# Folding the cosine and sine matrices into w_in with half-width pairs of matmuls, and one fold and one conversion at another place in the order

## The chip, the cores and the metric

The kernel runs on one core of a Trainium2 chip. The metric is device time of one execution in microseconds (us); lower is better. TensorE multiplies matrices into banks of PSUM; VectorE, ScalarE and GpSimd work on tiles element by element; SyncE issues the DMAs. Every engine works through its own queue in order, and instructions on different engines wait for each other through semaphores.

## The reference

```python
X = np.fft.fft(np.fft.fft(x, axis=1), axis=2)      # x: 8 x 3008 x 256, fp32
h = X.real.reshape(8 * 3008, 256) @ w_in           # w_in: 256 x 2048
g = np.where(h >= 1, h, np.where(h <= -1, 0, (h + 1) ** 2 / 4))
return g @ w_out                                   # w_out: 2048 x 256
```

## The kernel before

**The sequence transform.** The length 3008 is 64 x 47, and both factors are done as matmuls against cosine and sine blocks (stage1 for 47, stage2 for 64). The result of one batch lies in tiles pqh and pql, a value and what is left of it after rounding to fp32r, in three chunks (k = 0, 1, 2) of 482, 512 and 512 columns.

**The model dimension.** The second transform, of length 256, is never done on x. It is linear, so its cosine and sine matrices (`mats`, 256 rows by 128 columns each) are multiplied into w_in once, at the start: that is the fold, `fold_w_in`. w_in is 256 x 2048 and is folded in four quarters of 512 columns (f4 = 0 to 3), each for m = 0 (cosine) and m = 1 (sine). Each of these takes two fp32 matmuls (line 317), one for each half h of the 256 rows, into one bank `wps`. The result is split into wh (ScalarE, line 242) and wl (VectorE, line 244). For m = 1 row 0 holds something else: ScalarE copies it out (`drow`, line 323), it goes through DRAM to `delta`, and GpSimd clears the row in wh and wl with two memsets (line 335) after wl is done. The DRAM bytes of w_in and w_out arrive as 64-bit integers, so each piece (raw_0 to raw_15) is converted first: ScalarE `magnitude` (lines 279, 281), VectorE `assemble` (lines 290, 294).

**The units.** The large part of the kernel is 384 units. A unit is one batch, one chunk k and one f, which is 128 of the 2048 hidden columns. Its steps are:
- G: six fp32r matmuls (line 477) into two banks uv_i_0 and uv_i_1, out of three banks of that tag;
- U, H: VectorE us (line 492) and the sum and difference h (lines 500, 501); h has three buffers;
- R, Q: ScalarE relu (line 506) and square (line 510);
- L: VectorE larger (line 521), min and max in place in h;
- J: ScalarE gh (line 525); T and t: the two halves of GpSimd gl (line 530), four buffers each;
- M: twelve fp32r matmuls (line 631) into four banks acc, which are copied out after the last f of a visit (lines 616, 618).

Because uv_i_0 and uv_i_1 come from three banks, a unit's matmuls wait for us or h of the unit before or the one before that; and because h has three buffers, h_17 waits until gl_14 has read h_14. Batch 0 is done in two visits, f 0 to 7 and then f 8 to 15, with units 0 to 7 on k = 0, 8 to 15 on k = 1, 16 to 23 on k = 2, and 24 on with f from 8. So quarter 0 of w_in is needed by unit 0, quarter 1 by unit 4, quarter 2 by unit 24 and quarter 3 by unit 28.

**The order.** Up to unit 47 the order of every instruction on TensorE, ScalarE, VectorE and GpSimd is written out by hand in the text `WRITTEN` (lines 73 to 101). A letter is a step, the number its index, and a point with a number the next piece of a step begun before: e and v are the two parts of a conversion, b and a the folds for m = 1 and m = 0 (b2 the matmuls, b2.1 and b2.2 what follows on the other engines), p the pieces of batch 0's transform (p8 the matmul ny, p8.1 the copy nyt on ScalarE), o the split of w_out, d the first delta; G, U, H, R, Q, L, J, T, t, M as above. All engines share the text: each takes from it, in order, what is its own. The banks of a fold and of a transform come from `fft_bank`, which hands out acc0 to acc3 in turn for the first `EARLY_BANKS` calls and the bank "fft" after that, and from `fold_bank`, which gives quarters 2 and 3 a bank of uv.

Of the kernel before, what the change touches and what calls it, by code (L numbers as in the profile page):

```python
# [72 lines left out]
WRITTEN = """
f0 f1 f2 f3 f4 f5 f6 f7 p0 p1 w2 e0 e1 p0.1 p1.1 v0 v1 b0 b0.1 b0.2 a0 a0.1 a0.2 k0 p3 p3.1 p2 p2.1 p4 p5 p4.1 p6
p6.1 e4 v4 p5.1 p7 p7.1 e5 v5 n0 n0.1 p9 p9.1 p9.2 p8 e2 v2 p10 p10.1 p10.2 b1 b1.1 b1.2 d0 d0.1 o2 G0 G0.1 G1
U0 H0 U1 p8.1 e3 v3 o2.1 R0 a1 a1.1 a1.2 Q0 L0 o3 J0 G1.1 H1 p11 p11.1 G2 U2 G2.1 G3 G3.1 p11.2 H2 T0 t0 M0 R1
Q1 L1 R2 J1 T1 t1 Q2 e6 U3 H3 R3 L2 J2 l12 G4 G4.1 G5 U4 v6 H4 M1 Q3 R4 Q4 o3.1 G5.1 p12 G6 U5 L3 J3 L4 U6 T2
t2 M2 G6.1 G7 o6 J4 p12.1 T3 l8 t3 M3 T4 t4 o6.1 H5 R5 l9 Q5 p12.2 G7.1 H6 G8 U7 G8.1 R6 e7 Q6 L5 J5 T5 t5 H7
R7 v7 o7 L6 U8 M4 p13 o7.1 M5 Q7 p13.1 p13.2 L7 J6 J7 T6 t6 T7 t7 H8 p14 p14.1 G9 G9.1 G10 U9 H9 G10.1 U10
p14.2 R8 Q8 R9 Q9 e8 H10 L8 L9 J8 T8 R10 M6 G11 M7 G11.1 G12 M7.1 U11 M7.2 v8 U12 G12.1 M7.3 M7.4 Q10 J9 t8 M8  # L80
e9 H11 L10 J10 G13 U13 G13.1 T9 t9 H12 M9 T10 t10 v9 H13 R11 R12 Q11 Q12 L11 L12 R13 G14 U14 b2 G14.1 M10 G15
J11 T11 t11 Q13 L13 M11 J12 b2.1 T12 t12 H14 U15 b2.2 l10 G15.1 G16 R14 J13 l13 Q14 T13 t13 H15 a2 G16.1 L14
U16 H16 a2.1 R15 J14 M12 Q15 L15 a2.2 R16 J15 e12 Q16 T14 t14 G17 U17 G17.1 H17 R17 Q17 M13 v12 e13 G18 X0 U18
G18.1 G19 T15 t15 L16 H18 R18 v13 X1 L17 M14 M15 M15.1 J16 T16 Q18 t16 U19 M15.2 b3 L18 G19.1 G20 M15.3 H19
M15.4 M16 J17 T17 t17 y1 J18 b3.1 b3.2 U20 G20.1 G21 a3 H20 G21.1 R19 Q19 L19 U21 M17 T18 t18 H21 X3 G22 G22.1
M18 R20 J19 Q20 L20 R21 a3.1 U22 a3.2 G23 J20 Q21 l11 T19 y0 t19 H22 T20 t20 X2 y2 G23.1 l15 G24 M19 M20 U23
L21 H23 e11 R22 J21 Q22 T21 t21 v11 R23 o11 Q23 G24.1 o11.1 l14 L22 J22 T22 t22 q0 G25 q0.1 U24 H24 G25.1 R24
G26 Q24 U25 e10 L23 J23 H25 M21 G26.1 G27 L24 v10 J24 R25 T23 t23 o10 e14 M22 M23 o10.1 T24 t24 Q25 U26 G27.1
H26 G28 v14 q1 R26 o14 o14.1 M23.1 M23.2 U27 Q26 X5 H27 q1.1 G28.1 G29 X4 q2 L25 L26 J25 J26 T25 t25 U28 M23.3
M23.4 M24 H28 T26 t26 y3 y4 y5 R27 Q27 R28 q2.1 L27 Q28 J27 e15 G29.1 M25 G30 M26 U29 G30.1 U30 L28 J28 T27  # L90
t27 T28 t28 X6 H29 R29 Q29 H30 X7 R30 v15 Q30 L29 L30 o15 J29 J30 T29 t29 o15.1 G31 M27 G31.1 q3 M28 U31 H31
G32 U32 G32.1 H32 q3.1 R31 Q31 L31 R32 Q32 L32 J31 G33 U33 G33.1 q4 q4.1 J32 D0 G34 M29 T30 t30 M30 T31 t31 T32
t32 H33 R33 Q33 G34.1 G35 U34 H34 R34 Q34 G35.1 U35 H35 R35 L33 L34 J33 J34 T33 t33 D1 Q35 M31 M31.1 M31.2 M31.3
M31.4 G36 q5 G36.1 G37 q5.1 U36 U37 H36 M32 M33 y6 R36 Q36 L35 L36 J35 J36 y7 T34 t34 T35 t35 q6 G37.1 G38
G38.1 U38 q6.1 M34 G39 M35 H37 H38 R37 Q37 R38 Q38 L37 L38 J37 J38 G39.1 z0 U39 G40 U40 T36 t36 M36 z0.1 T37 t37 T38
t38 G40.1 H39 H40 R39 Q39 L39 R40 Q40 J39 G41 U41 G41.1 G42 q7 M37 H41 R41 Q41 L40 J40 M38 q7.1 U42 L41 G42.1
G43 z1 G43.1 U43 J41 T39 t39 M39 T40 t40 T41 t41 z1.1 q8 H42 H43 R42 Q42 M39.1 M39.2 M39.3 L42 R43 J42 G44 G44.1
G45 q9 Q43 q9.1 U44 M39.4 M40 H44 R44 Q44 q9.2 U45 L43 M41 q10 G45.1 J43 L44 q10.1 q10.2 J44 G46 G46.1 U46 T42
t42 H45 T43 R45 t43 Q45 T44 H46 M42 t44 L45 R46 J45 G47 Q46 T45 G47.1 U47 M43 t45 L46 H47 J46 T46 R47 t46 Q47
M44 L47 J47 M45 T47 t47 q11 q11.1 q11.2  # L100
"""
# [671 lines left out]
```

## Time and profile before

| | |
|---|---|
| runs | 1715.49, 1716.52, 1718.16 us, median 1716.52 us |
| profiled execution | 1716.01 us, of which the span of the trace 1713.9 us |
| TensorE busy | 1703.1 us, 99% |
| VectorE, ScalarE, GpSimd busy | 80%, 79%, 70% |
| granted TensorE clock | 1.00 |
| DMA | 72.6 MB, mean 42 GB/s |

The span runs from the first to the last instruction that the profiler saw. "Idle before" an instruction, in brackets behind a row of the timeline, is the time in which its engine stood still, with what ended it. A row with x4 stands for four instructions one after the other, and its time for the stretch that they fill. A fp32 matmul leaves two records, a fp32r matmul one; records overlap a little, so the step from one start to the next is the better price.

### The profile page before, as it was taken

Reading aid. Unit: us, or ns where it says so; the run is one execution under the profiler, and the core shown is the slowest. Engines: PE = TensorE matmul, PEld = TensorE weight load, DVE = VectorE, ACT = ScalarE, POOL = GpSimd, SP = SyncE. Lnnn points to the kernel's source line nnn. Section 1 sums busy time; section 2 is a strip of 40 time slices with the busy share of each in tenths; the row PEclk is TensorE's granted clock in tenths of the full one; section 3 lists DMA queues with packets and bytes.
Section 4 is the critical chain, followed back from the end, with each engine's and each line's share of the span. In section 5 each row is a group of like instructions: output and inputs, shape, how many; then the busy total and the mean of one; then the engine's idle time right before and its main releaser. Section 6 shows DMA issues by size and latency. Waiting matters only on the chain.

```text
span 1713.9 us, 21467 instructions
## 1 busy us (share of the span) xinstructions
PE 1703.1 (99%) x7764; PEld 1402.0 (82%) x7764; DVE 1378.0 (80%) x1683; ACT 1354.2 (79%) x1576; POOL 1202.1 (70%) x852
## 2 busy tenths in 40 slices
...
DMA packets 34221, 72.64 MB, mean 42 GB/s; under 512 B 5312, under 2 KB 10432, under 8 KB 34115
## 3 DMA queue, kind: packets, MB, share of 16 engines
...
q8 instruction: 61, 1.00, 0.2%
...
HBM read 43.44 MB, written 27.82 MB: 42 GB/s over the span
## 4 chain that ended last, share of the span: by engine, by line
PE 79%; POOL 9%; issue 4%; ACT 4%; DVE 3%; DMA 1%; SPq 0%; POOLq 0%; DVEq 0%; ACTq 0%
PE acc L631 49%; PE uv L477 25%; POOL gl L530 7%; PE s L357 2%; PE s L426 2%; DVE h L521 2%; ACT gh L525 1%; ACT a L510 1%; ACT a L506 1%; POOL y L150 1%; DVE h L501 1%; DVE h L500 0%; DMA raw<-in_moe_w_in_dram 0%; DVE us L492 0%; PE wps L317 0%
## 5 line engine op out<-in xcount | busy, mean ns | idle before, releaser
L530 POOL TENSOR_TENSOR gl<-h,gh 128x512 fp32r<-128x512 f32 (+1 forms) x764 | 1101.2, 1465 | 479.6 <-ACT gh L525 459.6
L521 DVE SCALAR_TENSOR_TENSOR h<-a,h 128x1024 f32<-128x1024 f32 (+1 forms) x385 | 561.3, 1459 | 237.9 <-ACT a L510 237.5
L525 ACT ACTIVATE gh<-h 128x1024 fp32r<-128x1024 f32 (+1 forms) x385 | 400.8, 1041 | 306.4 <-DVE h L521 276.0
L631 PE MATMUL acc<-gh,woh 128*128 128x512 f32 (+1 forms) x1536 | 606.1, 395 | 1.3 <-ACT o L616 1.2
L631 PE MATMUL acc<-gl,woh 128*128 128x512 f32 (+1 forms) x1536 | 601.8, 392 | 1.0 <-POOL gl L530 0.8
L631 PE MATMUL acc<-gh,wol 128*128 128x512 f32 (+1 forms) x1536 | 595.2, 388 | 0.0
L506 ACT ACTIVATE a<-h,half 128x1024 f32<-128x1024 f32 (+1 forms) x385 | 431.9, 1122 | 23.6 <-DVE h L501 20.8
L510 ACT ACTIVATE a<-a 128x1024 f32<-128x1024 f32 (+1 forms) x385 | 399.2, 1037 | 7.8
L631 PEld LDWEIGHTS acc<-gl,woh 128*128 128x128 f32 x1536 | 288.4, 188 | 63.1 <-POOL gl L530 2.4
L631 PEld LDWEIGHTS acc<-gh,wol 128*128 128x128 f32 x1536 | 289.2, 188 | 60.6 <-POOL wol L244 0.4
L631 PEld LDWEIGHTS acc<-gh,woh 128*128 128x128 f32 x1536 | 289.1, 188 | 58.3 <-ACT o L616 2.9
L500 DVE TENSOR_TENSOR h<-us,uv 128x512 f32<-128x512 f32 (+1 forms) x384 | 259.5, 676 | 65.6 <-POOL gl L530 22.4
L477 PE MATMUL uv<-pqh,wh 128*128 128x512 f32 (+1 forms) x768 | 306.1, 399 | 0.9 <-DVE h L501 0.7
L477 PE MATMUL uv<-pql,wh 128*128 128x512 f32 (+1 forms) x768 | 301.5, 393 | 0.0
L477 PE MATMUL uv<-pqh,wl 128*128 128x512 f32 (+1 forms) x768 | 298.5, 389 | 0.0
L492 DVE SCALAR_TENSOR_TENSOR us<-nyb,delta,uv 128x512 f32<-128x512 f32 (+1 forms) x384 | 278.8, 726 | 3.7 <-PE uv L477 3.4
L501 DVE TENSOR_TENSOR h<-us,uv 128x512 f32<-128x512 f32 (+1 forms) x384 | 256.3, 667 | 0.0
L477 PEld LDWEIGHTS uv<-pqh,wh 128*128 128x128 f32 x768 | 144.3, 188 | 39.1 <-DVE h L501 7.1
L477 PEld LDWEIGHTS uv<-pql,wh 128*128 128x128 f32 x768 | 144.2, 188 | 31.8
L477 PEld LDWEIGHTS uv<-pqh,wl 128*128 128x128 f32 x768 | 144.2, 188 | 30.7 <-issue 1.2
L378 ACT ACTIVATE z<-s 64x192 f32<-64x192 f32 x244 | 82.8, 340 | 3.8 <-PE s L357 0.4
L150 POOL TENSOR_TENSOR y<-x 128x384 f32<-128x384 f32 x56 | 80.5, 1439 | 1.1 <-PE s L357 1.1
...
## 6 DMA issues: line engine op xcount, KB each, us to landing
...
```

What stands on the lines that cost most here:

```text
L150: nc.gpsimd.tensor_tensor(y, t[:, 0], t[:, 1], op=ALU.add)
L378: nc.scalar.activation(dst, src, AF.Copy)
L477: nc.tensor.matmul(t[:, :n], w[m][:, cols], r[:, m, :n], start=(j == 0), stop=(j == 2))
L492: fixed(i, nc.vector.scalar_tensor_tensor(us, nyb[b, k][:, :n], d, uv[0], op0=ALU.mult, op1=ALU.add), 2)
L500: fixed(i, nc.vector.tensor_tensor(h[:, 0], us, v, op=ALU.subtract), 2)
L501: fixed(i, nc.vector.tensor_tensor(h[:, 1], us, v, op=ALU.add), 2)
L506: fixed(i, nc.scalar.activation(a[:, sl], h[:, sl], AF.Relu, bias=half, scale=0.5), 2)
L510: fixed(i, nc.scalar.activation(a[:, sl], a[:, sl], AF.Square), 2)
L521: fixed(i, nc.vector.scalar_tensor_tensor(h[:, sl], a[:, sl], 1.0, h[:, sl], op0=ALU.min, op1=ALU.max))
L525: fixed(i, nc.scalar.activation(gh[:, sl], h[:, sl], AF.Copy))
L530: fixed(i, eng.tensor_tensor(gl[:, sg], h[:, sg], gh[:, sg].bitcast(F32), op=ALU.subtract))
L631: nc.tensor.matmul(acc[:, :n], w[:, f, wc], g[:, sg], start=(first and j == 0), stop=(last and j == 2))
```

## The change

1. G_ORDER, the order of the 128 cosine frequencies, now has the even ones first and the odd ones last; stage1 writes z in the same order.
2. For quarters 1, 2 and 3 the two halves of w_in's rows are added and subtracted on GpSimd before the fold (`sum_w_in`, letter s, two operations of 128 x 512). An even frequency needs only the sum and an odd one only the difference, so each m takes two matmuls of 64 output columns, one into each half of the bank, in place of two of 128 that add up. Quarter 1's sum is written over the spent raw_5, quarters 2 and 3 use a tile `sums`.
3. Banks: quarters 2 and 3 take "fft" for m = 1 and uv for m = 0; EARLY_BANKS goes from 15 to 17, and quarter 1's m = 1 and m = 0 now take acc0 and acc1; acc1 is the bank of ny.
4. Order: quarter 1's fold (b1, a1) stands behind H0; the conversion e2 v2 is spread behind unit 0's first steps; nyt (p8.1) stands behind R0; b2 and a2 stand together behind M11, b3 and a3 together between uv_23_0 and uv_23_1.

```diff
-G_ORDER = np.arange(P).reshape(XC, GPC, 2, 2).transpose(0, 3, 1, 2).reshape(-1)
+G_ORDER = np.arange(P).reshape(XC, GPC, 2, 2).transpose(3, 0, 1, 2).reshape(-1)
...
-p6.1 e4 v4 p5.1 p7 p7.1 e5 v5 n0 n0.1 p9 p9.1 p9.2 p8 e2 v2 p10 p10.1 p10.2 b1 b1.1 b1.2 d0 d0.1 o2 G0 G0.1 G1
+p6 p6.1 e4 v4 p5.1 p7 p7.1 e5 v5 s1 n0 n0.1 p9 p9.1 p9.2 p8 p10 p10.1 p10.2 d0 d0.1 G0 e2 G0.1 U0 G1 H0 b1 a1 U1
...
-EARLY_BANKS = 15
+EARLY_BANKS = 17
...
-    def fold_bank(f4, name):
-        if f4 < 2:
-            return fft_bank(0, name)
+    def fold_bank(f4, m, name):
+        if f4 < 2 or m:
+            return fft_bank(f4 // 2, name)
         return ps.tile([P, CH], F32, tag="uv", name=name, bufs=3)
...
         for h in range(2):
-            nc.tensor.matmul(pt, mats[m][h], f32s[4 * f4 + h], start=(h == 0), stop=(h == 1))
+            if f4 not in sums:
+                nc.tensor.matmul(pt, mats[m][h], f32s[4 * f4 + h], start=(h == 0), stop=(h == 1))
+            else:
+                g = slice(h * P // 2, (h + 1) * P // 2)
+                nc.tensor.matmul(pt[g], mats[m][0][:, g], sums[f4][h], start=True, stop=True)
...
+    def sum_w_in(f4):
+        lo, hi = f32s[4 * f4], f32s[4 * f4 + 1]
+        if f4 == 1:
+            total = spent.pop(4 * f4 + 1).rearrange("p e two -> p (e two)")[:, :CH].bitcast(F32)
+            sums[f4] = total, hi
+        else:
+            if not spare:
+                spare.append(sb.tile([P, NC, P + 1], F32, tag="z", name="sums", bufs=1).rearrange("p c n -> p (c n)"))
+            sums[f4] = [spare[0][:, (2 * (f4 % 2) + h) * CH :][:, :CH] for h in range(2)]
+        for t, op in zip(sums[f4], (ALU.add, ALU.subtract)):
+            nc.gpsimd.tensor_tensor(t, lo, hi, op=op)
...
-                dst = z[m * NA : (m + 1) * NA, :, (2 * q + h) * 8 : (2 * q + h + 1) * 8]
+                dst = z[m * NA : (m + 1) * NA, :, (XC * h + q) * 8 : (XC * h + q + 1) * 8]
```

What this does to an engine's queue shows in three places. The first is VectorE from us_1 to h_1, before:

```order
L492 SCALAR_TENSOR_TENSOR us_1_309<-nyb_0_0_247,delta_75,uv_1_0_299 128x482
L290 SCALAR_TENSOR_TENSOR cv_2_260<-cv_2_260,raw_3_114 128x512
L294 SCALAR_TENSOR_TENSOR cv_2_260<-raw_3_114,cv_2_260 128x512
L244 TENSOR_TENSOR wl0_71<-wps_1_0_325,wh0_69 128x512
L521 SCALAR_TENSOR_TENSOR h_0_305<-a_0_308,h_0_305 128x2x482
L500 TENSOR_TENSOR h_1_340<-us_1_309,uv_1_1_336 128x482
```

And the same stretch of VectorE after (cv is the converted w_in, wps_1_0 and wps_1_1 the banks of quarter 1's fold; larger 0 is the row that writes h_0 with 128x2x482):

```order
L512 SCALAR_TENSOR_TENSOR us_1_302<-nyb_0_0_249,delta_75,uv_1_0_288 128x482
L292 SCALAR_TENSOR_TENSOR cv_2_279<-cv_2_279,raw_2_112 128x512
L296 SCALAR_TENSOR_TENSOR cv_2_279<-raw_2_112,cv_2_279 128x512
L244 TENSOR_TENSOR wl1_72<-wps_1_1_296,wh1_70 128x512
L244 TENSOR_TENSOR wl0_71<-wps_1_0_299,wh0_69 128x512
L541 SCALAR_TENSOR_TENSOR h_0_292<-a_0_295,h_0_292 128x2x482
L292 SCALAR_TENSOR_TENSOR cv_2_279<-cv_2_279,raw_3_114 128x512
L296 SCALAR_TENSOR_TENSOR cv_2_279<-raw_3_114,cv_2_279 128x512
L520 TENSOR_TENSOR h_1_342<-us_1_302,uv_1_1_338 128x482
```

The conversion of raw_2 and wl1 have come into this stretch, and the conversion of raw_3 has moved from ahead of larger 0 to between larger 0 and h_1.

The second place is TensorE around unit 15 and 16, first before:

```order
L631 MATMUL acc_8_3_734<-gl_11_831,woh_73 128x512
L477 MATMUL uv_15_1_871<-pqh_0_1_344,wh1_70 128x512
...
L477 MATMUL uv_16_0_875<-pql_0_2_585,wh0_69 128x512
L317 MATMUL wps_2_0_892<-cv_8_657,cm_68 128x512 x2
L477 MATMUL uv_16_1_895<-pqh_0_2_584,wh1_70 128x512
```

And after:

```order
L651 MATMUL acc_8_3_736<-gl_11_833,woh_73 128x512
L323 MATMUL wps_2_1_862<-sums_792,cm_68 64x512 x2
L323 MATMUL wps_2_0_865<-sums_792,cm_68 64x512 x2
L497 MATMUL uv_15_1_870<-pqh_0_1_346,wh1_70 128x512
...
L497 MATMUL uv_16_0_874<-pql_0_2_587,wh0_69 128x512
L497 MATMUL uv_16_1_893<-pqh_0_2_586,wh1_70 128x512
```

Both folds of quarter 2 stand directly behind M11 (the rows that write acc_8); before, one stood between uv_16_0 and uv_16_1 and the other ahead of M10.

The third place is GpSimd between unit 11 and unit 14, first before:

```order
L530 TENSOR_TENSOR gl_11_831<-h_11_750,gh_11_830 128x512 x2
L530 TENSOR_TENSOR gl_12_850<-h_12_770,gh_12_849 128x512 x2
L335 MEMSET wh1_70 1x512
L335 MEMSET wl1_72 1x512
L530 TENSOR_TENSOR gl_13_881<-h_13_790,gh_13_880 128x512 x2
L530 TENSOR_TENSOR gl_14_909<-h_14_860,gh_14_908 128x512 x2
```

And after:

```order
L351 TENSOR_TENSOR sums_792<-cv_8_659 128x512 x2
L550 TENSOR_TENSOR gl_11_833<-h_11_752,gh_11_832 128x512 x2
L550 TENSOR_TENSOR gl_12_852<-h_12_772,gh_12_851 128x512 x2
L550 TENSOR_TENSOR gl_13_880<-h_13_795,gh_13_879 128x512 x2
L355 MEMSET wh1_70 1x512
L355 MEMSET wl1_72 1x512
L550 TENSOR_TENSOR gl_14_912<-h_14_856,gh_14_911 128x512 x2
```

The two sums stand ahead of gl_11, and the two clears of row 0, which wait for wl1, stand ahead of gl_14 and no longer ahead of gl_13.

## Rows read from the trace of the kernel before

**Rows 1.** The page's busy times: us, share of the span, instructions.

```profile
PE 1703.1 (99%) x7764; PEld 1402.0 (82%) x7764; DVE 1378.0 (80%) x1683; ACT 1354.2 (79%) x1576; POOL 1202.1 (70%) x852
```

**Rows 2.** The windows: from:to, length, busy time by engine, clock, DMA.

```profile
250.00:1700.00 1450.00, 1448.74 (x6620) 1202.03 (x6619) 1163.40 (x1403) 1143.45 (x1295) 1027.45 (x713) 1.00 0.09 30
```

**Rows 3.** TensorE's waits: us in total, times, longest us.

```profile
PE acc L631 <- ACT o L616: 1.2, 2, 0.7
PE s L426 <- DVE wl L244: 1.1, 1, 1.1
```

**Rows 4.** Groups of instructions, the fold: busy us, mean ns, idle before.

```profile
L317 PE MATMUL wps<-cv,cm 128*128 128x512 f32 x32 | 15.2, 599 | 1.0 <-DVE cv L294 1.0
```

**Rows 5.** The timeline of TensorE, 22 to 37 us: start, us, instruction.

```profile
23.04 0.31 PE L389 MATMUL ny<-cs,z 128*24 128x64 f32 x2
23.28 1.16 PE L426 MATMUL s<-cs,z 128*128 128x128 f32 x8
24.28 1.88 PE L317 MATMUL wps<-cv,cm 128*128 128x512 f32 x4
26.09 1.10 PE L341 MATMUL dps<-half,drow 1*128 1x64 f32 x8
27.12 0.49 PE L477 MATMUL uv<-pqh,wh 128*128 128x482 f32 x1
...
32.82 1.16 PE L426 MATMUL s<-cs,z 128*128 128x128 f32 x8 [1.07 <-DVE wl L244]
...
35.15 0.45 PE L477 MATMUL uv<-pqh,wh 128*128 128x482 f32 x1
...
36.54 0.38 PE L631 MATMUL acc<-gh,woh 128*128 128x482 f32 x1
```

**Rows 6.** The timeline of VectorE, 28 to 37 us.

```profile
28.16 0.72 DVE L492 SCALAR_TENSOR_TENSOR us<-nyb,delta,uv 128x482 f32<-128x482 f32 x1
...
30.75 0.69 DVE L290 SCALAR_TENSOR_TENSOR cv<-cv,raw 128x512 uint32<-128x512 uint32 x1
...
32.76 1.17 DVE L521 SCALAR_TENSOR_TENSOR h<-a,h 128x964 f32<-128x964 f32 x1
...
34.40 0.65 DVE L501 TENSOR_TENSOR h<-us,uv 128x482 f32<-128x482 f32 x1
```

**Rows 7.** The timeline of ScalarE, 26 to 36 us.

```profile
27.82 0.20 ACT L392 ACTIVATE nyt<-ny 24x64 f32<-24x64 f32 x1
...
30.24 1.10 ACT L506 ACTIVATE a<-h,half 128x964 f32<-128x964 f32 x1 [1.11 <-DVE h L501]
```

**Rows 8.** The timeline of TensorE, 80 to 118 us.

```profile
81.55 1.88 PE L317 MATMUL wps<-cv,cm 128*128 128x512 f32 x4
...
88.58 0.39 PE L631 MATMUL acc<-gl,woh 128*128 128x512 f32 x1
...
91.61 1.88 PE L317 MATMUL wps<-cv,cm 128*128 128x512 f32 x4
...
113.67 0.39 PE L631 MATMUL acc<-gh,woh 128*128 128x512 f32 x1
```

**Rows 9.** The timeline of VectorE, 78 to 118 us.

```profile
82.27 2.35 DVE L521 SCALAR_TENSOR_TENSOR h<-a,h 128x1024 f32<-128x1024 f32 x2
...
92.84 2.97 DVE L521 SCALAR_TENSOR_TENSOR h<-a,h 128x1024 f32<-128x1024 f32 x1 [0.39 <-ACT a L510]
...
112.26 0.68 DVE L618 COPY o<-acc 128x512 f32<-128x512 f32 x1
```

**Rows 10.** The timeline of GpSimd, 74 to 104 us (second row: 86.2 to 87).

```profile
84.87 6.04 POOL L530 TENSOR_TENSOR gl<-h,gh 128x512 fp32r<-128x512 f32 x4 [3.83 <-ACT gh L525]
...
86.11 2.29 POOL L530 TENSOR_TENSOR gl<-h,gh 128x512 fp32r<-128x512 f32 x1
...
91.25 0.52 POOL L335 MEMSET wh<- 1x512 f32 x1 [0.34 <-DVE wl L244]
...
92.20 2.53 POOL L530 TENSOR_TENSOR gl<-h,gh 128x512 fp32r<-128x512 f32 x2
```

More of the change, by code (lines that the diff above doesn't have):

```diff
@@ L79 @@
[L79 to L93, printed above, removed]
@@ L99 @@
-t42 H45 T43 R45 t43 Q45 T44 H46 M42 t44 L45 R46 J45 G47 Q46 T45 G47.1 U47 M43 t45 L46 H47 J46 T46 R47 t46 Q47
-M44 L47 J47 M45 T47 t47 q11 q11.1 q11.2
+f0 f1 f2 f3 f4 f5 f6 f7 p0 p1 w2 e0 e1 p0.1 p1.1 v0 v1 b0 b0.1 b0.2 a0 a0.1 a0.2 k0 p3 p3.1 p2 p2.1 p4 p5 p4.1
+p6 p6.1 e4 v4 p5.1 p7 p7.1 e5 v5 s1 n0 n0.1 p9 p9.1 p9.2 p8 p10 p10.1 p10.2 d0 d0.1 G0 e2 G0.1 U0 G1 H0 b1 a1 U1
+R0 v2 p8.1 b1.1 b1.2 Q0 a1.1 a1.2 o2 L0 e3 v3 o2.1 J0 o3 G1.1 H1 p11 p11.1 G2 U2 G2.1 G3 G3.1 p11.2 H2 T0 t0 M0
+R1 Q1 L1 R2 J1 T1 t1 Q2 e6 U3 H3 R3 L2 J2 l12 G4 G4.1 G5 U4 v6 H4 M1 Q3 R4 Q4 o3.1 G5.1 p12 G6 U5 L3 J3 L4 U6 T2
@@ new lines @@
+t2 M2 G6.1 G7 o6 J4 p12.1 T3 l8 t3 M3 T4 t4 o6.1 H5 R5 l9 Q5 p12.2 G7.1 H6 G8 U7 G8.1 R6 e7 Q6 L5 J5 T5 t5 H7 R7
+v7 o7 L6 U8 M4 p13 o7.1 M5 Q7 p13.1 p13.2 L7 J6 J7 T6 t6 T7 t7 H8 p14 p14.1 G9 G9.1 G10 U9 H9 G10.1 U10 p14.2 R8
+Q8 R9 Q9 e8 H10 L8 L9 J8 T8 R10 M6 G11 M7 G11.1 G12 M7.1 U11 M7.2 v8 U12 G12.1 M7.3 M7.4 Q10 J9 t8 M8 e9 H11 L10
+J10 G13 U13 G13.1 T9 t9 H12 M9 T10 t10 v9 s2 H13 R11 R12 Q11 Q12 L11 L12 R13 G14 U14 G14.1 M10 G15 J11 T11 t11
+Q13 L13 M11 J12 T12 t12 H14 U15 b2 a2 l10 G15.1 G16 R14 J13 l13 Q14 a2.1 T13 t13 H15 a2.2 G16.1 L14 U16 H16 b2.1
@@ new lines @@
+R15 J14 M12 Q15 L15 b2.2 R16 J15 e12 Q16 T14 t14 G17 U17 G17.1 H17 R17 Q17 M13 v12 e13 G18 X0 U18 G18.1 G19 T15
+t15 L16 H18 R18 v13 X1 L17 M14 M15 M15.1 J16 T16 Q18 t16 U19 M15.2 L18 G19.1 G20 M15.3 H19 M15.4 M16 J17 T17 t17
+y1 J18 U20 G20.1 G21 H20 G21.1 R19 Q19 L19 U21 M17 T18 t18 s3 H21 X3 G22 G22.1 M18 R20 J19 Q20 L20 R21 U22 G23
+b3 a3 J20 Q21 l11 T19 y0 t19 H22 a3.1 T20 t20 X2 y2 G23.1 l15 a3.2 G24 M19 M20 U23 b3.1 L21 b3.2 H23 e11 R22 J21
+Q22 T21 t21 v11 R23 o11 Q23 G24.1 o11.1 l14 L22 J22 T22 t22 q0 G25 q0.1 U24 H24 G25.1 R24 G26 Q24 U25 e10 L23
@@ new lines @@
+J23 H25 M21 G26.1 G27 L24 v10 J24 R25 T23 t23 o10 e14 M22 M23 o10.1 T24 t24 Q25 U26 G27.1 H26 G28 v14 q1 R26 o14
+o14.1 M23.1 M23.2 U27 Q26 X5 H27 q1.1 G28.1 G29 X4 q2 L25 L26 J25 J26 T25 t25 U28 M23.3 M23.4 M24 H28 T26 t26 y3
+y4 y5 R27 Q27 R28 q2.1 L27 Q28 J27 e15 G29.1 M25 G30 M26 U29 G30.1 U30 L28 J28 T27 t27 T28 t28 X6 H29 R29 Q29
+H30 X7 R30 v15 Q30 L29 L30 o15 J29 J30 T29 t29 o15.1 G31 M27 G31.1 q3 M28 U31 H31 G32 U32 G32.1 H32 q3.1 R31 Q31
+L31 R32 Q32 L32 J31 G33 U33 G33.1 q4 q4.1 J32 D0 G34 M29 T30 t30 M30 T31 t31 T32 t32 H33 R33 Q33 G34.1 G35 U34
@@ new lines @@
+H34 R34 Q34 G35.1 U35 H35 R35 L33 L34 J33 J34 T33 t33 D1 Q35 M31 M31.1 M31.2 M31.3 M31.4 G36 q5 G36.1 G37 q5.1
+U36 U37 H36 M32 M33 y6 R36 Q36 L35 L36 J35 J36 y7 T34 t34 T35 t35 q6 G37.1 G38 G38.1 U38 q6.1 M34 G39 M35 H37
+H38 R37 Q37 R38 Q38 L37 L38 J37 J38 G39.1 z0 U39 G40 U40 T36 t36 M36 z0.1 T37 t37 T38 t38 G40.1 H39 H40 R39 Q39
+L39 R40 Q40 J39 G41 U41 G41.1 G42 q7 M37 H41 R41 Q41 L40 J40 M38 q7.1 U42 L41 G42.1 G43 z1 G43.1 U43 J41 T39 t39
+M39 T40 t40 T41 t41 z1.1 q8 H42 H43 R42 Q42 M39.1 M39.2 M39.3 L42 R43 J42 G44 G44.1 G45 q9 Q43 q9.1 U44 M39.4
```

20 lines of the change are left out of this document (9 added, 11 removed).

## The prediction

> **What bounds the kernel now.** I read the page's busy table first: TensorE works 1703.1 of 1713.9 us [rows 1]. The windows say where the other 11 us are: between 250 and 1700 us TensorE is busy 1448.7 of 1450 us at a granted clock of 1.00 [rows 2], so of the whole idle time all but 1.3 us lies in the first 250 us and in the last 14. The change touches nothing past about unit 30 except the order of rows in the cosine matrix, so the question is what happens before 140 us. There TensorE sets the end: a microsecond taken off its queue is a microsecond of time, if the next matmul in the queue finds its operands and its bank ready. The table of waits shows how near the other engines run: behind the first one, for the warm-up, its longest entries are 1.2 us in two waits and 1.1 us in one [rows 3]. They are short, but not because the others are fast; they end just before TensorE asks. So for every fold that moves I asked two things: how much TensorE work goes, and which result was being made behind the old fold.
>
> **Work of the fold.** One quarter's fold was four fp32 matmuls, each recorded as two records, 32 records in all [rows 4]. The four records that start at 24.28 are followed by the next group at 26.09: 1.81 us, of which some 1.75 is the four records (0.43 each) [rows 5]. A quarter costs two such groups, 3.5 us. A half-width matmul has as many moving columns (512) and the same contraction, so I give each of its records the same 0.43 us. If both halves of a pair run one behind the other nothing is saved; if they run side by side a pair costs half, 1.75 us less per quarter. No row of before has two matmuls in different column halves, so the saving lies between 0 and 1.75, and below nothing only by the price of changing the shape. For that the nearest rows are the narrow matmuls at 23.04 (24 columns of the array): their two records take 0.24 us until 23.28 where the full-width ones after them go at 1.00/8 = 0.125 each for twice the columns, so 0.13 would do and the change of shape costs 0.11 for the way there and back [rows 5]. I take the middle: the second record of one half beside the first record of the next half, eight records in five steps, 5 x 0.43 = 2.15 in place of 3.5, **-1.3 us a quarter**. Quarters 2 and 3 give -2.6; quarter 1 stands in the first term below.
>
> The Trainium skill, TensorE: Matmul & The Clock Gate, Part 3 (Packing small matmuls), says that matmuls at different tile positions of the array overlap, and start and end strictly in order. By it a pair would cost one matmul, 5.2 us over three quarters; no run here shows it yet. Against the change speaks TensorEngine Tiling (Array Packing), Key Properties, of the Trainium skill: changing the tiling mode drains TensorE. The narrow matmuls agree in sign, with 0.11 us there and back.
>
> **Start: +1.25 (from -1.75 to +2.5).** The fold at 24.28 no longer stands ahead of unit 0, so uv of unit 0 starts at 25.3 in place of 27.12, and us_0 at 26.4 in place of 28.16 [rows 5, 6]: 1.8 us of lead. Then it is used up. The first relu runs at 28.5 instead of 30.24; nyt, which had run at 27.82, now stands behind it in ScalarE's queue [rows 7], about 29.6, and the second fold (m=0) takes the bank that nyt frees: it cannot start before 29.65, though its turn in TensorE's queue comes at 28.75 (idle 0.9). It ends about 31.0; wh0 on ScalarE follows square 0, at 32.05; wl0 on VectorE at 32.1 to 32.75; larger 0 behind it at 32.75, which is where it is today (32.76) [rows 6]. Behind larger 0 VectorE now has the two operations of raw_3's assembly (2 x 0.69, as at 30.75) which had stood ahead of it. So h_1 ends at 36.35 in place of 35.05, and the matmul of uv_3_0 at 35.15, which needs h_1's bank, and M0 at 36.54 [rows 5] come 1.25 later. Gains inside it: the 1.07 us wait for wl goes [rows 5] and quarter 1's cheaper fold; both are in the chain, none is added again. If relu 0 and wl0 are early enough, all 1.75 us of lead stay (lower end); if nyt and wl0 slip by one more relu (1.10), +2.5.
>
> **M11: +1.9 (0.9 to 3.3).** Quarter 2's first fold stood at 81.55, ahead of M10 and M11; now it comes behind M11. M11's sixth matmul, at 88.58, needs the second half of gl_11; gl_11 begins at 84.87, and its second half runs from 86.11 for 2.29 us, to 88.40, 0.18 us ahead [rows 8, 10]. It hangs on larger 11 and gh_11, not on TensorE, so it doesn't come earlier: 1.75 - 0.18 = 1.6. The two sums (2 x 1.3 on GpSimd) fit into its idle 3.83 us ahead of 84.87, but there larger 11 and 12 run, two in 2.35 us, while GpSimd stands still [rows 9, 10]; beside a GpSimd operation one larger took 2.97 [rows 9]. I add 0.3 for larger 11; the ends are gl's halves at 1.3 apiece, and larger 11 at 2.97.
>
> **uv_16_1: +0.95 (0 to 1.6).** The other fold stood at 91.61 between uv_16_0 and uv_16_1 [rows 8]. Under it VectorE made h_15, whose end frees the bank of uv_16_1: from uv_15_1's end 0.5 and 2 x 0.65 us, 1.86 with the switch, against uv_16_0's three matmuls and a start of 0.93.
>
> **uv_19_0: +1.8 (0 to 4.3).** Here the change adds a wait to a queue. GpSimd's two clears of row 0 (0.52 us each, at 91.25) wait for wl1 [rows 10]; with the fold behind M11 and its last step behind larger 15, they now stand ahead of gl_14 and not of gl_13. From the end of h_15: VectorE wl0 0.65, larger 14 1.2, us_16 0.7, h_16 1.3, larger 15 1.2, wl1 0.65; GpSimd clears 1.0, gl_14 2.5 (like the 2.53 at 92.20) [rows 10]; VectorE h_17, in h_14's buffer, 1.3: 10.5 us. TensorE from uv_16_1 on has 39 matmuls, 9.0 us at 0.23, then uv_19_0, which needs h_17. 1.5 us short, and I take 1.8, since a larger may meet GpSimd; with one at 2.97 and gl at 1.5 a half it is over 4.
>
> **M16 and units 24 to 26: +2.4 (0.5 to 4).** Fold 3's first group (the third of four like the two of fold 2 [rows 8]), ahead of M16, covered the copy of o_15_1, 112.26 to 112.94, which frees acc_16_2 for its matmul at 113.67 [rows 8, 9]: slack 0.73, fold 1.75, +1.0. Fold 3 now stands as a whole between uv_23_0 and uv_23_1, and m=0 holds a bank of uv until its wl0 is done: 0.3 + 0.6 + 0.7 us after its end, uv_23_1 is 0.7 long, so uv_24_0 waits 0.9; 0.5 for the same further on.
>
> **Sum.** 1.25 + 1.9 + 0.95 + 1.8 + 2.4 = 8.3; less 2.6: **+5.7 us**. The profiled execution took 1716.0 (span 1713.9); it would be 1721.7. The three runs shown have a median of 1716.5, 0.5 above it, so I forecast 1722.2.
>
> **Rivals.**
> *The engines stop meeting (faster).* Place: units 11 to 19. Larger took 2.97 us beside GpSimd and 1.2 with GpSimd idle (two in 2.35); gl's second half 2.29 beside larger, and two halves 2.53 where they met it least [rows 9, 10]. If the new places of clears and sums keep the two apart, gl_11 and the chain to h_17 each end 1 to 1.8 us earlier than I have them, and every wait above is hidden again; the lead of the start isn't lost either. Then only the work counts: 3 x -1.3 = -3.9, 1712.6, and 1711.3 with pairs side by side. It decides at larger 11 and gl_11: below 1.4 us each. For it: these engines have 20 to 30% idle time [rows 1]. Against it: the sums are put just where larger 11 had GpSimd quiet. 22%.
> *Half-width matmuls run one behind the other.* Nothing is saved, +8.3: 1724.8. For it: no row shows an overlap. 14%.
> *Half of the waits.* The terms at the start and at uv_19_0 hang on chains of six to eight steps, each with 0.1 us of slack; without these two 8.3 - 3.05 - 2.6 = +2.65, 1719.2. 22%.
> *The forecast*, with its own range of 1719.5 to 1726: 42%.
>
> **Numbers.** What a measurement of this kernel can tell from no change is 0.2%, 3.4 us: faster is below 1713.1, slower above 1720.0. Slower: 0.42 and 0.14, less 0.02 for the forecast's lower edge, 0.54; same 0.22 and 0.02, 0.24; faster 0.22. The range leaves out a tenth on either side: below, most of the faster case stays in (1711.5); above, the ends of M11 and uv_19_0 (+1.4 and +2.5) with no saving, 1728.7, about 1729.
>
> **What would show it.** Records of the half-width matmuls in a profile of after: their starts 0.43 apart (serial) or pairs at one start. In the waits of TensorE: new lines for gl of unit 11 (about 1.9), for h at uv_16_1 and uv_19_0 (about 2.7 in all), for the copy of o (1.0). At the start, M0 at 37.8. Idle time of TensorE before 250 us some 7 to 8 us above before's. I am wrong if M0 comes ahead of 36 us, if gl_11's wait is missing, or if TensorE has new waits past 250 us.

## The result, and the profile after

The changed kernel takes 1727.29 us (median of 6 runs, 1726.92 to 1729.52) against 1716.16 us on the same chip (6 runs, 1715.24 to 1718.16): **+11.1 us, ratio 1.0065, 95% interval [1.0052, 1.0078]**. That is slower, as forecast, inside the range (to 1729.0) but near its end, and nearly twice as far as the forecast of +5.7. The profiled execution took 1727.8 us, its span is 1726.0 us.

The page's busy times, where [rows 1] stood:

```profile
PE 1703.4 (99%) x7764; PEld 1401.0 (81%) x7764; DVE 1378.3 (80%) x1683; ACT 1354.9 (79%) x1576; POOL 1209.5 (70%) x858
```

TensorE is busy for as long as before (1703.1), though the fold has become cheaper: what the fold saves goes into matmuls at a lower clock and into the first matmul behind each wait, which counts as busy for longer (both below). So in the page's account the whole loss is idle time. TensorE's waits, us in total, times, longest; the nine lines of this view, of which six are shown, add up to 17.9 us (all eight of before, of which [rows 3] shows two, to 6.5):

```profile
PE uv L497 <- DVE h L521: 9.2, 8, 3.5
PE acc L651 <- POOL gl L550: 2.0, 3, 1.2
PE acc L651 <- ACT o L636: 1.6, 2, 0.9
...
PE acc L651 <- DVE o L638: 1.2, 1, 1.2
PE wps L323 <- ACT nyt L412: 1.2, 1, 1.2
PE uv L497 <- DVE us L512: 0.9, 1, 0.9
```

Eight times TensorE waits for h, where there had been two waits of 0.7 us together. They lie early: between 250 and 1710 us the idle time is 2.1 us, in a stretch of 1460 us, and the timelines below place all but small ones ahead of 152 us.

```profile
250.00:1710.00 1460.00, 1457.88 (x6663) 1209.08 (x6662) 1168.42 (x1408) 1148.24 (x1301) 1033.83 (x717) 1.00 0.09 30
```

**The fold.** TensorE's timeline at the start, and at quarter 2's fold (start, us, instruction, x records), where [rows 5, 8] had 1.88 for every four records:

```profile
25.60 0.49 PE L497 MATMUL uv<-pqh,wh 128*128 128x482 f32 x1
...
27.79 0.64 PE L323 MATMUL wps<-raw,cm 128*64 128x512 f32 x1
27.80 0.64 PE L323 MATMUL wps<-cv,cm 128*64 128x512 f32 x1
28.27 0.59 PE L323 MATMUL wps<-raw,cm 128*64 128x512 f32 x1
28.28 0.59 PE L323 MATMUL wps<-cv,cm 128*64 128x512 f32 x1
30.03 0.64 PE L323 MATMUL wps<-raw,cm 128*64 128x512 f32 x1 [1.16 <-ACT nyt L412]
...
37.73 0.48 PE L497 MATMUL uv<-pqh,wh 128*128 128x482 f32 x1 [3.55 <-DVE h L521]
38.56 0.60 PE L497 MATMUL uv<-pqh,wh 128*128 128x482 f32 x1
39.76 0.61 PE L651 MATMUL acc<-gh,woh 128*128 128x482 f32 x1
...
93.37 0.40 PE L651 MATMUL acc<-gl,woh 128*128 128x512 f32 x1
93.70 1.94 PE L323 MATMUL wps<-sums,cm 128*64 128x512 f32 x8
95.56 0.50 PE L497 MATMUL uv<-pqh,wh 128*128 128x512 f32 x1
95.90 0.39 PE L497 MATMUL uv<-pqh,wl 128*128 128x512 f32 x1
```

The same stretch around one full-width group of before, whose own row stands in [rows 8]:

```profile
81.32 0.39 PE L477 MATMUL uv<-pql,wh 128*128 128x512 f32 x1
...
83.50 0.39 PE L477 MATMUL uv<-pqh,wl 128*128 128x512 f32 x1
```

The records of the two halves start 0.01 us apart: they run side by side, both of their passes. A quarter's eight records take 1.86 us, from 93.70 to 95.56, so a pair's four take 0.93, about what one full-width matmul took (two records of 0.43). By the Trainium skill (TensorE: Matmul & The Clock Gate, Part 3), matmuls at different tile positions run concurrently. This trace agrees. The queue gains a little less than the records show, since 0.1 us is lost on each side of them: from the last matmul ahead to the second one behind are 2.53 us (93.37 to 95.90), less two usual steps of 0.23 a price of 2.07 for the quarter. The same count for a group of before gives 1.72 (81.32 to 83.50), 3.44 for a quarter. So 1.4 us are saved a quarter, 4.1 for three.

**The start.** Unit 0 begins 1.5 us earlier (25.60 for 27.12 in [rows 5]) and M0 3.2 us later (39.76 for 36.54). TensorE stands still for 3.55 us ahead of uv_3_0, which needs h_1. VectorE and GpSimd there:

```profile
26.69 0.72 DVE L512 SCALAR_TENSOR_TENSOR us<-nyb,delta,uv 128x482 f32<-128x482 f32 x1 [0.69 <-PE uv L497]
...
32.95 2.27 DVE L541 SCALAR_TENSOR_TENSOR h<-a,h 128x964 f32<-128x964 f32 x1
...
37.03 0.65 DVE L521 TENSOR_TENSOR h<-us,uv 128x482 f32<-128x482 f32 x1
```

```profile
32.90 1.29 POOL L244 TENSOR_TENSOR wol<-cv,woh 128x512 fp32r<-128x512 f32 x1 [0.21 <-ACT woh L242]
```

Larger 0 starts where it was forecast (32.75) but takes 2.27 us in place of 1.17 [rows 6], with GpSimd's split of w_out beside it, which had run at 29.06 before, beside other work. Behind the wait the granted clock falls: two windows, the wait and what follows it.

```profile
34.00:37.70 3.70, 0.18 (x1) 0.00 (x0) 3.67 (x6) 2.12 (x3) 1.56 (x3) 1.00 0.23 57
37.70:42.00 4.30, 4.27 (x12) 3.56 (x13) 4.17 (x7) 4.04 (x4) 1.10 (x1) 0.60 0.00 0
```

A mean of 0.60 over these 4.3 us, after TensorE had been idle for 3.5: eight matmuls go at 0.40 us instead of 0.22, some 1.5 us.

**The middle.** TensorE's waits from 85 to 150 us, one by one:

```profile
89.68 0.50 PE L651 MATMUL acc<-gl,woh 128*128 128x512 f32 x1 [0.55 <-POOL gl L550]
91.88 0.50 PE L651 MATMUL acc<-gl,woh 128*128 128x512 f32 x1 [1.23 <-POOL gl L550]
98.08 0.50 PE L497 MATMUL uv<-pqh,wh 128*128 128x512 f32 x1 [0.85 <-DVE h L521]
...
108.90 0.50 PE L497 MATMUL uv<-pqh,wh 128*128 128x512 f32 x1 [1.52 <-DVE h L521]
...
119.80 0.51 PE L651 MATMUL acc<-gh,woh 128*128 128x512 f32 x1 [1.19 <-DVE o L638]
...
134.37 0.50 PE L497 MATMUL uv<-pqh,wh 128*128 128x512 f32 x1 [1.25 <-DVE h L521]
144.57 0.48 PE L497 MATMUL uv<-pqh,wh 128*128 128x482 f32 x1 [0.88 <-DVE us L512]
146.33 0.48 PE L497 MATMUL uv<-pqh,wh 128*128 128x482 f32 x1 [0.84 <-DVE h L521]
```

In order: gl_11 in M11, h_15 ahead of uv_16_1, h_17 ahead of uv_19_0, the copy of o_15_1 in M16, h_22 ahead of uv_23_1, and two at units 24 and 25 (a smaller one, 0.37, follows at 151.08). GpSimd shows the reasons for the third and the fifth:

```profile
83.85 3.54 POOL L351 TENSOR_TENSOR sums<-cv 128x512 f32<-128x512 f32 x2
87.59 6.74 POOL L550 TENSOR_TENSOR gl<-h,gh 128x512 fp32r<-128x512 f32 x4 [0.20 <-ACT gh L545]
...
104.04 0.52 POOL L355 MEMSET wh<- 1x512 f32 x1 [6.16 <-DVE wl L244]
...
125.98 2.57 POOL L351 TENSOR_TENSOR sums<-cv 128x512 f32<-128x512 f32 x2
128.50 2.29 POOL L550 TENSOR_TENSOR gl<-h,gh 128x512 fp32r<-128x512 f32 x1
```

It stands still for 6.16 us for the two clears, with gl_14 behind them; and quarter 3's sums run ahead of gl_19, whose end frees h_22's buffer.

### The profile page after: what moved, and what is told of

Its sections match the earlier page's. It is cut to its first block, busy times and chain, and to the rows that moved or that the text cites. A ratio compares the mean times of both kernels' runs of the same rounds, so it can differ in the third digit from the quotient of the medians.

```text
span 1726.0 us, 21481 instructions
## 1 busy us (share of the span) xinstructions
PE 1703.4 (99%) x7764; PEld 1401.0 (81%) x7764; DVE 1378.3 (80%) x1683; ACT 1354.9 (79%) x1576; POOL 1209.5 (70%) x858
## 4 chain that ended last, share of the span: by engine, by line
PE 76%; POOL 7%; issue 3%; ACT 3%; DVE 2%; DMA 0%; POOLq 0%; ACTq 0%; DVEq 0%
PE acc L651 48%; PE uv L497 24%; POOL gl L550 7%; PE s L377 2%; PE s L446 2%; DVE h L541 1%; ACT gh L545 1%; ACT a L530 1%; ACT a L526 1%; POOL y L150 0%; DVE h L521 0%; DMA x<-in_x_dram 0%; DVE h L520 0%; ACT o L636 0%; DVE gl L550 0%
## 5 line engine op out<-in xcount | busy, mean ns | idle before, releaser
L520 DVE TENSOR_TENSOR h<-us,uv 128x512 f32<-128x512 f32 (+1 forms) x384 | 259.5, 676 | 74.3 <-POOL gl L550 29.6
```

The source lines that it names most:

```text
L520: fixed(i, nc.vector.tensor_tensor(h[:, 0], us, v, op=ALU.subtract), 2)
```

## The experiments

To compare stages, this table gives how much later than in the kernel before the first matmul of M0, M8, M12, M18 and M23 starts in each profiled execution (us; the shift of the first nys matmul at 20.19 us, 0.2 to 0.8, is taken off: e10 and e11, whose order up to there is that of before, have it too). Of the times, only the ratio to before on the same chip is compared; with four runs it is known to about 0.0016, some 3 us, so single moves of 1 us are read from the stages.

| kernel | M0 | M8 | M12 | M18 | M23 | median, us (runs) | before | ratio [95%] |
|---|---|---|---|---|---|---|---|---|
| after | 3.0 | 2.6 | 4.7 | 4.3 | 10.4 | 1727.29 (6) | 1716.16 | 1.0065 [1.0052, 1.0078] |
| e8 start as before | 0.0 | 0.0 | 2.1 | 1.7 | 7.9 | 1723.88 (5) | 1716.11 | 1.0044 [1.0032, 1.0057] |
| e9 middle as before | 2.9 | 2.6 | 2.6 | 2.9 | 2.8 | 1718.56 (11) | 1716.11 | 1.0013 [1.0004, 1.0022] |
| e1 full width | 3.9 | 2.9 | 8.0 | 7.5 | 14.0 | 1728.47 (4) | 1715.08 | 1.0081 [1.0063, 1.0098] |
| e2 wol later | 1.9 | 1.5 | 3.5 | 3.1 | 9.2 | 1726.39 (4) | 1715.08 | 1.0061 [1.0046, 1.0076] |
| e3 nyt first | 3.5 | 3.2 | 5.2 | 4.8 | 10.9 | 1727.94 (4) | 1715.08 | 1.0082 [1.0065, 1.0100] |
| e4 raw_3 later | 1.1 | 3.8 | 7.5 | 7.1 | 13.2 | 1727.25 (4) | 1716.29 | 1.0066 [1.0053, 1.0080] |
| e5 clears early | 3.4 | 2.6 | 6.2 | 3.4 | 9.6 | 1725.68 (4) | 1715.08 | 1.0058 [1.0043, 1.0073] |
| e6 s3 later | 3.5 | 2.3 | 5.9 | 5.5 | 12.0 | 1729.22 (4) | 1716.11 | 1.0075 [1.0062, 1.0089] |
| e10 pairs, old places | 0.0 | 0.0 | 0.1 | 3.2 | 3.2 | 1719.38 (11) | 1716.11 | 1.0018 [1.0009, 1.0027] |
| e11 the same, no sums | 0.0 | 0.0 | -0.6 | 0.0 | 0.0 | 1714.76 (11) | 1716.29 | 0.9996 [0.9987, 1.0005] |
| e12 after, no sums | 3.6 | 3.7 | 5.0 | 4.6 | 9.5 | 1727.96 (4) | 1716.29 | 1.0066 [1.0051, 1.0080] |
| e13 four moves | 1.9 | 1.5 | 1.5 | -1.3 | 6.0 | 1720.69 (10) | 1716.29 | 1.0025 [1.0016, 1.0034] |

**Each half of the change alone (e8, e9).**

```diff
e8: the order's start up to H1 is that of before again, and EARLY_BANKS = 15
    -p6 p6.1 e4 v4 ... s1 n0 ... e3 v3 o2.1 J0 o3 G1.1 H1
    +p6 p6.1 e4 v4 ... n0 ... b1 b1.1 b1.2 ... a1 a1.1 a1.2 ... H1
e9: from p11 on the order of before, without s2 s3; its fold_bank
```

> The start up to H1 (order, banks, quarter 1 full width) is that of the kernel before; everything from there on, with quarters 2 and 3 in half-width pairs, is that of the changed kernel. Theory (the loss is a sum of local waits: 2.6 us at the start, 8.5 us between M10 and M22): the start's 2.6 us go, 1724.7 us, M8 within 0.3 us of before and M24 about 8 us behind it. Rival (the waits of the middle come from the late start, which took the other engines' lead): the middle gets better with it, below 1720 us.

> The other half: the start of the changed kernel with quarter 1 in half-width pairs, and from G1.1 on the order and the full-width folds of the kernel before. Theory (local waits): only the start's 2.6 us stay, 1718.8 us, M24 still 2.6 us behind. Rival (the late start makes the middle wait): above 1722 us. Rival (a lead is regained later): 1716.2 us.

1723.88 and 1718.56: both as the theory of local waits has it. Over before they are 7.8 and 2.5 us, together 10.2 of the 11.1. In e8 M8 is level with before and M23 7.9 behind, in e9 M8 is 2.6 behind and nothing is added or regained. The late start doesn't make the middle wait.

**The width alone (e1).**

```diff
-                nc.tensor.matmul(pt[g], mats[m][0][:, g], sums[f4][h], start=True, stop=True)
+                nc.tensor.matmul(pt, mats[m][0], sums[f4][h], start=(h == 0), stop=(h == 1))
```

> The changed kernel's order and sums, but each fold matmul full width (128 columns, the two of a pair adding up in one bank, so w_in comes out wrong); only the width differs. Theory (the halves overlap, 0.95 us a pair instead of 1.75; waits elsewhere make the kernel slow): quarters 2 and 3 cost 1.6 us more each, quarter 1's extra 1.6 us disappears in the wait ahead of uv_3_0, so 1727.3 + 3.3 = 1730.6 us. Rival (changing the tile shape and what it drains eats the overlap): 1727.3 us.

The median, 1728.47, lies between the two; by the ratio it is 0.0016 above after, 2.7 us, with intervals that overlap, so the time doesn't decide. The profile does:

```profile
95.61 4.16 PE L322 MATMUL wps<-sums,cm 128*128 128x512 f32 x8
...
134.94 3.60 PE L322 MATMUL wps<-sums,cm 128*128 128x512 f32 x8
```

Quarter 2's eight records take 4.16 us here (part of them at a lower clock, below) and quarter 3's 3.60 at the full clock, against 1.94 in half width (the row at 93.70 above). At M23 e1 is 3.6 us behind after, but some 1.6 of that are the lower clock behind M11's waits, which after doesn't have. Shape changes don't eat the overlap: they take the 0.2 us a quarter counted above.

**The moves at the start (e2, e3, e4).**

```diff
e2: -o2 L0 e3 v3 o2.1 J0 o3 ... H2 T0 t0 M0      +o2 L0 e3 v3 J0 o3 ... H2 T0 o2.1 t0 M0
e3: -U1 R0 v2 p8.1 b1.1                          +U1 p8.1 R0 v2 b1.1
e4: -e3 v3 o2.1 J0 o3 G1.1 H1 ... Q1 L1 R2       +e3 o2.1 J0 G1.1 H1 ... Q1 L1 v3 o3 R2
```

> Only GpSimd's first split of w_out (wol, 1.29 us) moves, from beside larger 0 to between the two halves of gl_0. Theory (larger 0 took 2.27 us and not 1.17 because GpSimd ran beside it, and the long wait of TensorE that follows lowers its clock): larger 0 back at about 1.2 us, h_1 1.1 us earlier, the wait ahead of uv_3_0 3.55 -> 2.45: 1726.2 us with the fall of the clock, 1724.4 us if the shorter wait no longer brings it about. Rival (larger 0 is long for another reason): 1727.3 us.

> Only ScalarE's copy nyt moves, ahead of relu 0, so that the bank of quarter 1's second fold is free 1.2 us earlier. Theory (that fold's wait for nyt is not on the path: wh0 stands behind square 0 on ScalarE, and TensorE waits for h_1 anyway): the wait for nyt goes (1.16), the wait ahead of uv_3_0 grows by as much, 1727.3 us. Rival (the wait for nyt is on the path, as the prediction's sum had it): 1726.1 us.

> Only the assembly of raw_3 (two operations on VectorE, 1.35 us) and its split on ScalarE move, from ahead of h_1 to behind larger 1. Theory (the prediction's term: that assembly holds h_1, which holds uv_3_0): the wait ahead of uv_3_0 goes from 3.55 to 2.2 us, and it stays won: 1725.9 us. Rival (VectorE is full until 60 us, 34.9 busy of 36 us between 24 and 60 us, so the 1.35 us come back at us_3 and h_3): 1727.3 us.

e2: larger 0 is back at 1.15 us and the wait at 2.43; M0 and M8 come 1.1 us earlier. That GpSimd's split makes larger 0 long is shown, and the clock falls all the same (0.59 in the 4.2 us behind the wait):

```profile
33.14 1.15 DVE L539 SCALAR_TENSOR_TENSOR h<-a,h 128x964 f32<-128x964 f32 x1
```

e3: the wait for nyt is gone, and the one ahead of uv_3_0 is 4.80 us, all of it and more; nothing is won. M8 is 0.6 us further behind than in after, since the clock stays down longer (0.57 over 5.7 us):

```profile
37.80:43.50 5.70, 5.67 (x16) 4.77 (x17) 5.57 (x9) 5.45 (x6) 2.27 (x2) 0.57 0.00 1
```

e4: the wait falls to 2.21 us, M0 comes 1.9 us earlier than in after, and the clock doesn't fall there. Then it is all given back:

```profile
36.76 0.48 PE L495 MATMUL uv<-pqh,wh 128*128 128x482 f32 x1 [2.21 <-DVE h L519]
42.34 0.49 PE L495 MATMUL uv<-pqh,wh 128*128 128x482 f32 x1 [0.71 <-DVE us L510]
43.70 0.48 PE L495 MATMUL uv<-pqh,wh 128*128 128x482 f32 x1 [0.43 <-DVE h L519]
45.56 0.48 PE L649 MATMUL acc<-gl,woh 128*128 128x482 f32 x1 [0.50 <-POOL gl L548]
47.66 0.49 PE L649 MATMUL acc<-gl,woh 128*128 128x482 f32 x1 [1.18 <-POOL gl L548]
```

2.8 us of new waits, M8 1.2 us later than in after. The rival was right: VectorE has no gap there, and what is pushed behind one result is ahead of the next.

**The clears and quarter 3's sums (e5, e6).**

```diff
e5: -a2.1 T13 t13 H15 a2.2 G16.1 L14 U16 H16 b2.1 R15 J14 M12 Q15 L15 b2.2
    +a2.1 b2.1 T13 t13 H15 a2.2 b2.2 G16.1 L14 U16 H16 R15 J14 M12 Q15 L15
e6: -T18 t18 s3 H21 ... b3 a3 J20 Q21 l11 T19 y0 t19 H22    +T18 t18 H21 ... b3 a3 J20 Q21 l11 T19 y0 t19 s3 H22
```

> Only quarter 2's last steps move: wh1, delta and wl1 with the two clears on GpSimd right behind wh0 and wl0, so the clears no longer wait behind larger 15 ahead of gl_14. Theory (the clears hold gl_14, gl_14 holds h_17, h_17 holds uv_19_0): the wait of 1.5 us ahead of uv_19_0 goes, at most 0.4 of it comes back elsewhere: 1725.6 us. Rival (gl_14 is late by itself): 1727.3 us.

> The changed kernel with one step moved: GpSimd makes quarter 3's sums behind both halves of gl_19, not ahead of them. Theory (the sums hold gl_19, gl_19 holds h_22, h_22 holds uv_23_1): the wait of 1.25 us ahead of uv_23_1 goes, part of it comes back as uv_24_0's wait for the bank of the fold until wl0: 1726.3 us. Rival (it all comes back there): 1727.3 us.

e5: uv_19_0 doesn't wait any more, and from M12 to M18 the kernel gains 2.8 us on before where after gains 0.4. That the clears hold gl_14 is shown by the stages; the ratio (1.0058) is 0.0007 lower, less than the runs can tell. e6 did more than its expectation says: the sums now stood behind the fold in the text, so quarter 3's fold was made in full width, and its sums were made for nothing. The wait ahead of uv_23_1 is gone and uv_24_0 waits 0.71 us for wl:

```profile
132.63 3.59 PE L318 MATMUL wps<-cv,cm 128*128 128x512 f32 x8
137.64 0.49 PE L495 MATMUL uv<-pqh,wh 128*128 128x482 f32 x1 [0.71 <-DVE wl L242]
```

From M18 to M23 it loses 6.5 us where after loses 6.1, though the full width costs some 1.4 more; so about 1 us of wait went, in line with the theory, but the time (a ratio of 1.0075) settles nothing, since two things were changed.

**Pairs without the new order, with and without sums (e10, e11, e12).**

```diff
e10 (order of before): -G14 U14 b2 G14.1 M10 ... Q13 L13 M11    +v9 s2 ... G14 U14 G14.1 M10 ... Q13 L13 b2 M11
                       -M15.2 b3 L18 G19.1 G20 M15.3 H19        +v13 s3 ... M15.2 L18 G19.1 G20 M15.3 b3 H19
e11 and e12: sums[f4] = f32s[4 * f4], f32s[4 * f4 + 1], and no nc.gpsimd.tensor_tensor
```

> The kernel before, its order and its start, with half-width pairs for quarters 2 and 3 only, at nearly the old places: s2 behind v9 and s3 behind v13; b2 directly ahead of M11 (it must wait for its sums), b3 one step later behind M15.3; a2 and a3 where they were. Theory (pairs save 0.8 us each, 3.3 us for the four; a fold that stays ahead of M11, uv_16_1 and M16 covers the same results as before): 1716.2 - 2.2 = 1714.0 us, at best 1712.9. Rival (VectorE bounds this stretch, 19.25 busy of 20 us between 100 and 120 us, so TensorE's saved work turns into waits): 1716.2 us.

> As the run with pairs for quarters 2 and 3 at the old places, instruction for instruction, but without the four sums on GpSimd: the pairs read the two halves of w_in themselves (so w_in comes out wrong). Theory (the sums, 2.6 to 3.5 us of GpSimd a quarter beside a busy VectorE, cost more than the pairs save): M17 and M18 ahead of before by 2 to 3 us, 1713.5 us. Rival (VectorE's chain bounds this stretch whatever GpSimd does, and TensorE's saved time turns into waits for it): 1716 us or more.

> The changed kernel without any sums on GpSimd (the pairs read the halves of w_in themselves, so w_in comes out wrong); order unchanged. Theory (in this order the sums of quarters 1 and 2 lie in idle time, those of quarter 3 hold gl_19): the 1.25 us ahead of uv_23_1 go and most waits stay, 1725.9 us. Rival (the sums make the larger steps long and so cause the other waits too): 1722 us or less.

e10 is 3.3 us slower than before, where 2.2 faster was expected, and slower than its rival had it too. Three of the four groups are as cheap as in after (1.08 us for four records); the one ahead of M16 takes 1.71, since its second half starts only when its sum is done. With the 0.1 us on each side a group costs 1.21 us where it cost 1.72, so the four would save 2.0 us, and not the 3.3 of the expectation. Up to M12 nothing is lost, but of the 1.0 us that quarter 2 saves nothing arrives either, and by M18 3.2 are lost. GpSimd's row and what waits for it on VectorE (h_19, for gl_16):

```profile
108.71 3.46 POOL L349 TENSOR_TENSOR sums<-cv 128x512 f32<-128x512 f32 x2 [4.61 <-PE acc L649]
112.12 6.02 POOL L548 TENSOR_TENSOR gl<-h,gh 128x512 fp32r<-128x512 f32 x4
```

```profile
115.66 0.69 DVE L518 TENSOR_TENSOR h<-us,uv 128x512 f32<-128x512 f32 x1 [1.81 <-POOL gl L548]
```

Quarter 3's two sums take 3.46 us ahead of gl_16, more than its pairs save. e11 takes the sums away and leaves all else: the 3.2 us go, M23 is level with before. The gain of the pairs is still not there: TensorE's waits are now

```profile
PE uv L486 <- DVE h L510: 1.5, 4, 0.5
...
PE acc L640 <- POOL gl L539: 0.9, 3, 0.5
```

and its time, 1.5 us below before, can't be told from no change. So both sides had a part: the sums cost about 3.2 us, and of the 2.0 us that the pairs save in TensorE's queue none reaches M23, since the results that it waits for come no sooner. VectorE, which makes h, is busy for 19.3 of the 20 us from 100 to 120; that its queue is the reason fits this row, but isn't shown, because b2 and b3 also stand one step later than in the kernel before.

```profile
100.00:120.00 20.00, 19.83 (x84) 14.28 (x83) 19.32 (x24) 16.57 (x20) 14.04 (x12) 1.00 0.38 124
```

In that window TensorE's busy time stands first behind the length, then the weight loads', VectorE's, ScalarE's and GpSimd's. e12, the order of after without sums, keeps most waits (3.54 ahead of uv_3_0, 1.51 ahead of uv_19_0). M11's first and the one ahead of uv_23_1 go, the 0.88 for us shrinks to under 0.2, and uv_24_0 waits 0.52 for wl. From M8 to M23 it loses 5.8 us where after loses 7.8, so in this order the places cost most, and the sums some 2.0 us. The time is that of after, which is no contradiction: in the profiled execution the clock stayed down longer behind the first wait (M8 1.1 us later than in after), and 2 us are less than four runs can tell.

**Four moves at once (e13).** o2.1 as in e2, the clears as in e5, and

```diff
-Q13 L13 M11 J12 T12 t12 H14 U15 b2 a2 l10     +Q13 L13 b2 a2 M11 J12 T12 t12 H14 U15 l10
-M15.2 L18 G19.1 G20 M15.3 H19                 +M15.2 M15.3 L18 G19.1 G20 H19
```

> The changed kernel with four moves at once, one for each wait: wol's split between the halves of gl_0; quarter 2's fold ahead of M11, not behind it; wh1, wl1 and the clears right behind wh0 and wl0; the copy of o_15_1 ahead of larger 18. Theory (the waits are separate, each has its own cause): larger 0 -1.1, M11 1.8 -> 0.3, uv_19_0 -1.5, M16 -1.0, together 1727.3 - 5.1 = 1722.2 us. Rival (VectorE or GpSimd is full there, and each wait comes back at the next place): above 1725 us.

1720.69 us, 4.4 over before, below the 1722.2 that was expected: up to M18 the waits were separate. M11 and M16 don't wait, uv_19_0 waits 0.29, and at M18 the kernel is 1.3 us ahead of before, 5.6 ahead of after. It then loses 7.3 us until M23; 2.1 are quarter 3's fold, and the rest is waits and what each costs beyond its idle time: 2.44 us ahead of uv_23_1, since h_22 stands behind gl_19 and that behind quarter 3's sums, then 0.86, 0.85 and 0.38. The wait ahead of uv_23_1 was 1.25 in after, so 1.2 of the 5.6 us come back there, as the rival has it for every wait:

```profile
130.12 0.50 PE L495 MATMUL uv<-pqh,wh 128*128 128x512 f32 x1 [2.44 <-DVE h L519]
```

No version is faster than the kernel before by more than the runs can tell.

## Why the prediction was right, and where its sum was off

- **What bounds the kernel: right.** All but about 1 us of the loss lies ahead of 155 us, and it came as idle time of TensorE behind results that had been covered by the old folds. Ahead of 250 us there are 10.7 us more of it than before, where 7 to 8 had been forecast.
- **That the range held is in part luck.** Its end, 1729, was worked out from no saving in the fold and from M11 and uv_19_0 at their worst. None of the three came; other terms took their place.
- **Work of the fold: -1.4 us a quarter for -1.3, by another way.** Both halves run side by side in both passes, where the forecast had them overlap only in part, eight records in five steps; and 0.1 us is lost on each side, where it had 0.11 for both in a bound and nothing in its 2.15. The two errors nearly cancel (2.07 measured), which is luck. The rival with halves one behind the other is refuted.
- **Start: +2.6 at M8, not +1.25.** The chain was right step by step (larger 0 forecast at 32.75, seen at 32.95; nyt at 29.6, seen at 29.78). Two sizes were missed: larger 0 at 2.27 us, because GpSimd's split of w_out now runs beside it (1.1 us, e2), which the chain of VectorE and ScalarE alone didn't show; and some 1.5 us of lower clock behind the wait that the forecast itself had. Together these are 3.9; 1.3 are regained by M8, because waits that before had between M0 and M8 (0.52 at 43.27 the longest) don't come. The idle 0.9 put down to nyt (1.16 seen) was in the chain but cost nothing (e3). That raw_3 stands ahead of h_1 is true, but it isn't what costs: moved away, its time comes back (e4).
- **M11 1.9: 1.78 seen. uv_16_1 0.95: 0.85. uv_19_0 1.8: 1.52**, with the cause shown by e5. **M16 1.0: 1.19.**
- **Units 24 to 26: 1.4 forecast, 3.3 seen (1.25, 0.88, 0.84, 0.37).** This is the step that failed. It counted the bank of wps_3_0, and not that the two sums of quarter 3, issued on GpSimd ahead of gl_19, hold h_22; without the sums (e12) the 1.25 goes, most of the 0.88 too, and 0.52 comes. The same question was asked for quarter 2's sums and answered rightly (GpSimd had been idle again for 0.20 us when gh_11 let gl_11 start; still, M11's first wait goes without the sums, e12); for quarter 3's it wasn't asked.
- **Each wait costs more than its idle time.** From the matmul at 106.99 to the one at 108.90 are 1.92 us, 1.69 more than the usual step, for 1.52 us of idle time, and the first matmul behind it takes 0.1 longer. Over the waits from M8 to M23 that is some 2 us, and the forecast had nothing for it: the largest of the missed terms.
- **The sum at M23.** 2.6 at the start, 8.5 of idle time more than before behind M8, 2.0 beyond it, less 2.7 for the two folds: 10.4, as the table has. The forecast had 1.25, 7.05, nothing and 2.6.
- **Rivals.** Engines that stop meeting: larger 11 took 1.25 us, below its point of 1.4, but gl_11's halves 2.03 and 2.25 and larger 12 with the sums beside it 2.3; refuted. Half of the waits: refuted, all came.
